# First batch of a gated-attention and MoE kernel: u of all chunks from SyncE's queue, W1's second fourth held back behind chunk 2's attention

## Chip, cores, metric

One core of a Trainium2 chip. The metric is the device time of one execution in microseconds (us); the kernel is tuned, and TensorE is busy 99% of its span.

## The reference

```python
B, S, D, DQK = 8, 3008, 256, 64
scores = (1 / S) * z @ z.T                  # per batch
out = u * (maximum(scores, 0) ** 2 @ v)     # gated attention
x = out.reshape(B * S, D)
h = x @ w_in                                # 256 x 2048
y = (h * sigmoid(1.702 * h)) @ w_out        # 2048 x 256
```

## The kernel before

A batch is worked through in six chunks of 512 rows: scores, ReLU on ACT, square on VectorE, then attention on TensorE. As the scores are symmetric, a square that one chunk has made is transposed by a DMA (into `tt`) for use in another chunk. "The transposes of (m, n)" are squares made for chunk m's rows and chunk n's columns. Chunk 4's attention of the first batch is mixed with the first up-projection (`hg`), which needs W1 in fp16.

```python
pu = tile_pool(name="pu", bufs=2)         # u as loaded, u as turned
pa = tile_pool(name="pa", bufs=1)         # squares "a" (26 buffers), transposed "tt" (14)

def load_u(b, i):
    eng = pool if b or i else sp          # chunk 0 of batch 0 from SyncE, the rest from POOL
    ...
    for k in range(P // QW):              # 4 DMAs of 128 KB
        eng.dma_start(uq[...], src[...])

def turn_u(b, i):                         # VectorE, in order with its squares
    dve.transpose(ut, UQ.pop((b, i)))     # the gate multiplies attention by ut

def turn_unit(b, i, jp, a):               # SyncE, in order
    sp.dma_start_transpose(TT[b, i, cj][...], a)

def load_w(k):
    if k == 0:                            # POOL waits here until chunk 1's gate is made
        hold = const.tile([P, 1], F16, name="hold")
        pool.tensor_copy(hold, XT[0, 1][:, 0, :1])
    if k < 4:                             # 512 KB, a fourth of W1
        WS[k] = pw.tile([P, NCC, DFF // 4], F32, name="wst", tag="y")   # two buffers
        pool.dma_start(WS[k], moe_w_in...)
    ...

# (chunk, step of its attention): what is issued there
LOAD0 = {(1, 14): 2, (2, 12): 3, (2, NJ + 20): 4, (4, 8): 5}           # chunks of u
LOADW = {(2, 16): 0, (2, 30): 1, (3, 9): 2, (3, 41): 3, ...}           # W1, W2
CASTW = {(3, 8): 0, (3, 40): 1, (4, 8): 2, (4, 14): 3}                 # ACT, W1 to fp16
```

POOL and SyncE each issue in order and stop at the first DMA whose buffer or data is not ready: from 14 to 100 us POOL waited 21.5 us for buffers of u, and from 9 to 66 us SyncE waited 23.4 us for squares.

Of the kernel before, what the change touches and what calls it, by code (L numbers as in the profile page):

```python
# [10 lines left out]
F16 = mybir.dt.float16  # L11
P = 128
# [3 lines left out]
def kernel(  # L16
# [39 lines left out]
    dve, act, pe, sp, pool = nc.vector, nc.scalar, nc.tensor, nc.sync, nc.gpsimd  # L56

    const = ctx.enter_context(tc.tile_pool(name="const", bufs=1))
# [20 lines left out]
    ZT, V16, UQ, UT, XT, unit, TT = {}, {}, {}, {}, {}, {}, {}  # L79
# [41 lines left out]
    def first_cast(g, by_act=False):  # L121
        m = g % CB * CB
        for c in range(2):
            dst, src = ZT["st"][g // CB][:, m:m + CB, c, :], ZT["f"][g // CB][:, m:m + CB, :]
            if by_act:
                act.activation(dst, src, AF.Copy, scale=1.0)  # L126
            else:
                dve.tensor_copy(dst, src)

    def first_zt(g):  # L130

        z2 = ZT["st"][g // CB][:, g % CB * CB:(g % CB + 1) * CB]
        zp = ZP[g] if g in ZP else ps1.tile([P, CB, P], F16, name="zp", tag="ps1")
        for k in range(CB):
            pe.transpose(zp[:, k, :], z2[:, k, :, :], ident)  # L135

        def copies():
            zt = ZT[0][:, g * CB:(g + 1) * CB, :].rearrange("d n p -> d (n p)")
            nb = CB if g < NCH - 1 else CB - 1
            dst = zt[:, :nb * P].rearrange("d (p n) -> d p n", n=nb)  # L140
            src = zp[:, :nb, :].rearrange("d n p -> d p n")
            if g in (0, 2, 3):
                act.activation(dst, src, AF.Copy, scale=1.0)  # L143
            else:
                dve.tensor_copy(dst, src)
            if nb < CB:
                dve.tensor_copy(zt[:, nb * P:], zp[:, nb, :])

        return copies


    def load_z(b):
        ZT[b] = pz.tile([P, NJ, P], F16, name="ZT", tag="ZT")
        for n0 in range(0, NJ, NU):
            zst = pw.tile([P, NU, 2, DQK], F16, name="zst", tag="y")
            full = min(NU, NJ - 1 - n0)
            src = z[b, n0 * P:(n0 + full) * P].rearrange("(n p) d -> p n d", p=P)
            pool.dma_start(zst[:, :full, 0, :], src)
            if full < NU:
                for h in range(2):  # L160
                    pool.dma_start(zst[h * SREM:(h + 1) * SREM, full, 0, :], z[b, S0:S])
            pool.tensor_copy(zst[:, :, 1, :], zst[:, :, 0, :])
            sp.dma_start_transpose(ZT[b][:, n0:n0 + NU], zst.rearrange("p n c d -> p (n c d)"))
# [21 lines left out]
    def width(i):  # L185
        return CH if i < NCH - 1 else LAST

    def load_u(b, i):
        eng = pool if b or i else sp
        n = width(i)  # L190
        uq = pu.tile([P, CH // QW, QW, NCC], F32, name="uq", tag="uq")
        src = u[b, i * CH:i * CH + n].rearrange("(q t) c -> t q c", t=QW)
        for k in range(P // QW):
            cs = slice(k * NCC * QW, (k + 1) * NCC * QW)
            eng.dma_start(uq[k * QW:(k + 1) * QW, :n // QW].rearrange("t q c k -> t q (c k)"), src[:, :, cs])  # L195
        UQ[b, i] = uq

    def turn_u(b, i):
        n = width(i)
        ut = pu.tile([P, NCC, CH // QW, QW], F32, name="ut", tag="ut")  # L200
        UT[b, i] = ut
        dve.transpose(
            ut[:, :, :n // QW, :].rearrange("p k q t -> p q k t"),
            UQ.pop((b, i))[:, :n // QW].rearrange("p q c k -> p q k c"),
        )
# [114 lines left out]
    def full(b):  # L320

        return NCH - 2 if b < B - 1 else NCH - 1
# [106 lines left out]

    def load_w(k):  # L430

        if k == 0:
            hold = const.tile([P, 1], F16, name="hold")
            pool.tensor_copy(hold, XT[0, 1][:, 0, :1])
        if k < 4:
            WS[k] = pw.tile([P, NCC, DFF // 4], F32, name="wst", tag="y")
            pool.dma_start(WS[k], moe_w_in.rearrange("(p k) f -> p k f", k=NCC)[:, :, k * DFF // 4:(k + 1) * DFF // 4])
        else:
            fs = slice((k - 4) * CB, (k - 3) * CB)
            pool.dma_start(W2[:, fs], moe_w_out.rearrange("(fo p) c -> p fo c", p=P)[:, fs])  # L440

    def cast_w(k):
        act.activation(W1[:, :, k * DFF // 4:(k + 1) * DFF // 4], WS.pop(k), AF.Copy, scale=1.0)  # L443
# [154 lines left out]
    def pieces(b, i):  # L598
# [22 lines left out]
    LOAD0 = {(1, 14): 2, (2, 12): 3, (2, NJ + 20): 4, (4, 8): 5}  # L621
    TURN = {(1, NJ + 4): 2, (2, NJ + 4): 3, (4, NJ + 4): 4, (5, 8): 5}
    LOADW = {
        (2, 16): 0, (2, 30): 1, (3, 9): 2, (3, 41): 3, (4, 28): 4, (4, 34): 5, (4, 40): 6, (5, 0): 7,
    }
    CASTW = {(3, 8): 0, (3, 40): 1, (4, 8): 2, (4, 14): 3}
    LOAD = {(3, NJ + 20): 4, (4, NJ + 5): 5}
# [13 lines left out]
    def take(b, n):  # L641
        for post_ in scores(b, [queue.pop(0) for _ in range(n)]):
            post_()

    def fill(b):
        assert not queue
        queue.extend(u_ for i in range(NCH) for u_ in pieces(b, i))
# [24 lines left out]
    keep_warm(1)  # L672
    copies()
    ZP[3] = ps1.tile([P, CB, P], F16, name="zp", tag="ps1")
    load_u(0, 1)

    for b in range(B):
        nup = NCH * NFG
        more = b + 1 < B
        sched = SCHED0 if b == 0 else SCHED if more else SCHED_LAST  # L680
        turn, load = (TURN, LOAD) if b else (TURN0, LOAD0)
        head = 0
        for i in range(NCH):
            host = b + 1 if more and i == NCH - 1 else b
            if host > b:
                fill(host)
                LATE.append(host)
            for n, step in enumerate(attend(b, i, b == 0 and i < 2)):
                if b == 0 and i == 0 and n == 5:
                    load_u(0, 0)  # L690
                if b == 0 and i == 0 and n == 2:
                    copies = first_zt(3)
                if b == 0 and i == 0 and n == 3:
                    copies()
                if b == 0 and i == 0 and n in FIRST_CAST:
                    first_cast(FIRST_CAST[n], True)
                if b == 0 and i == 0 and n in FIRST_ZT:
                    first_zt(FIRST_ZT[n])()
                if (i, n) in turn:
                    turn_u(b, turn[i, n])  # L700
                if i == 3 and n in (3, 26) and LAST2:
                    LAST2.pop(0)()
                if (i, n) in load:
                    load_u(b, load[i, n])
                if b == 0 and (i, n) in CASTW:
                    cast_w(CASTW[i, n])
                if b == 0 and (i, n) in LOADW:
                    load_w(LOADW[i, n])
                if more and (i, n) == (NCH - 2, 2 if b else 16):
                    load_z(b + 1)  # L710
                if b == 0 and i == NCH - 1 and n in (8, 30, 42):
                    wsums.pop(0)()
                take(host, sched[i].get(n, 0))
                if i == full(b) and n >= HEAD and (n - HEAD) * LAGY // (2 * NJ - 10) >= head and head < LAGY:
                    up_group(b, head)
                    head += 1
                step()
        late.sort(key=lambda t: t[0])
        if more:
            for i in range(2):  # L720
                load_u(b + 1, i)
            for n0 in range(0, NJ, VB):
                load_v(b + 1, n0)
        prods = products(b)
        for q in range(head, nup):
            if more and q in (head + 14, head + 20):
                k = int(q == head + 20)
                turn_u(b + 1, k)
                load_u(b + 1, k + 2)
            up_group(b, q)  # L730
            if b == 0 and q == head + 3:
                wsums.pop(0)()
            product(b, *prods.pop(0))
            if q >= 30 and q % 2 and late:
                late.pop(0)[1]()
        steps = [lambda kp=kp: product(b, *kp) for kp in prods]
        for step in steps:
            step()
            for sum_ in [SUMS.pop(0) for _ in range(min(len(SUMS), 1 + (len(SUMS) > 4)))]:
                sum_()  # L740
            for _, turn_it in [late.pop(0) for _ in range(min(len(late), 1 + (len(steps) < 10)))]:
                turn_it()
        LATE.clear()
        if more:
            while late:
                late.pop(0)[1]()
            take(b + 1, 2)
# [30 lines left out]
```

## Time and profile before

| | us |
|---|---|
| median of 6 executions (range) | 1180.55 (1180.33 to 1186.32) |
| the profiled execution | 1180.55, span 1178.7 |
| TensorE idle from 14 to 100 us | 0.24 |

Five of the six lie within 0.31 us of each other and one is 5.7 us longer. The lines of the profile that carry the reading stand in the prediction. One more is needed for what comes later. It is the view of the source line that issues the transposes, from 14 to 80 us: the shortest, median and longest time from issue to landing.

```profile
DMA to landing us min/median/max: 3.1/5.2/8.9
```

### The profile page before, as it was taken

How to read it: one execution, taken by the hardware profiler on the slowest of the kernel's cores; microseconds unless marked ns; L12 is line 12 of the kernel's file. 1: busy time of each engine (PE TensorE's matmuls, PEld its weight loads, DVE VectorE, ACT ScalarE, POOL GpSimd, SP SyncE). 2: the span in 40 equal slices, each digit the busy share in tenths (PEclk: the TensorE clock that was granted, in tenths of full speed). 3: DMA queues.
4: the chain of work that ended last, by engine and by line, in shares of the span. 5: the costliest groups of instructions: out<-in, count | busy, mean ns of one | idle time of the engine just before them, and what ended most of it. 6: DMA issues, size and time to landing. Idle time of an engine off the chain costs nothing.

```text
span 1178.7 us, 23495 instructions
## 1 busy us (share of the span) xinstructions
PE 1172.5 (99%) x9238; PEld 667.2 (57%) x9238; DVE 870.7 (74%) x1455; ACT 849.6 (72%) x1033; POOL 222.1 (19%) x313
## 2 busy tenths in 40 slices
PE   9999999999999999999999999999999999999998
PEld 3446664466644675446654467544674446744566
DVE  6779866878758786587875878658786587764776
ACT  7888874688746887478864787647876478772785
POOL 5243101231012310132101431014100241001000
PEclk9999999999999999999999999999999999999999
DMA  9998679877698677976879668896578965796023
GB/s 226 217 120 125 133 116 160 91 112 135 106 156 100 108 135 130 150 91 95 147 128 149 94 93 157 139 137 94 94 135 135 141 106 97 127 158 127 1 37 73
DMA packets 449696, 143.66 MB, mean 122 GB/s; under 512 B 414640, under 2 KB 443056, under 8 KB 449584
## 3 DMA queue, kind: packets, MB, share of 16 engines
q1 hardware_dynamic: 392160, 99.80, 51.2%
q0 software_dynamic: 56064, 41.04, 23.1%
q8 instruction: 72, 1.18, 0.4%
q10 hardware_dynamic: 1360, 1.31, 0.4%
q14 instruction: 40, 0.33, 0.1%
HBM read 60.29 MB, written 24.64 MB: 72 GB/s over the span
## 4 chain that ended last, share of the span: by engine, by line
PE 99%; ACT 1%; issue 0%; DVE 0%
PE o L358 40%; PE hg L399 27%; PE st L523 23%; PE sc L235 6%; PE st L526 1%; PE yp L497 1%; PE w L99 0%; ACT rl L256 0%; ACT W L443 0%; ACT gf L407 0%; PE zp L135 0%; ACT ZT L143 0%; ACT zst L126 0%; DVE y L544 0%; DVE nil L75 0%
## 5 line engine op out<-in xcount | busy, mean ns | idle before, releaser
L407 ACT ACTIVATE gf<-hg 128x1024 f32<-128x1024 f32 (+1 forms) x384 | 385.5, 1004 | 113.6 <-PE hg L399 98.3
L256 ACT ACTIVATE rl<-sc 128x1024 f16<-128x1024 f32 (+1 forms) x301 | 287.5, 993 | 145.4 <-PE sc L235 101.2
L358 PEld LDWEIGHTS <-V 64*128 64x128 f16 (+1 forms) x4052 | 217.7, 94 | 253.9 <-issue 11.8
L399 PE MATMUL hg<-xt,W 128*128 128x512 f16 (+1 forms) x1408 | 354.6, 374 | 0.2
L358 PE MATMUL o<-a,V 64*128 64x512 f16 (+3 forms) x2240 | 296.0, 368 | 0.0
L411 DVE TENSOR_SCALAR gt<-gf 128x1024 f16<-128x1024 f32 (+1 forms) x288 | 203.0, 705 | 114.0 <-ACT gf L407 112.8
L195 POOL DMA_DIRECT2D uq<-in_u_dram x188 | 125.2, 674 | 751.8 <-PE sc L235 527.5
L270 DVE TENSOR_TENSOR a<-rl 128x1024 f16<-128x1024 f16 (+1 forms) x266 | 177.6, 670 | 112.3 <-ACT rl L256 111.0
L358 PE MATMUL o<-tt,V 64*128 64x512 f16 (+1 forms) x1510 | 232.2, 377 | 0.0
L399 PEld LDWEIGHTS <-W 128*128 128x128 f16 x1536 | 149.4, 98 | 125.6 <-issue 2.6
L523 PEld LDWEIGHTS <-WT 128*128 128x128 f16 x1472 | 139.1, 98 | 45.1
L523 PEld LDWEIGHTS <-W 128*128 128x128 f16 x1104 | 104.7, 98 | 32.2
L235 PE MATMUL sc<-ZT 64*128 64x512 f16 (+3 forms) x688 | 115.5, 357 | 0.5 <-ACT ZT L143 0.3
L409 ACT ACTIVATE gt<-gf 128x1024 f16<-128x1024 f32 (+1 forms) x96 | 98.9, 1030 | 3.0
L540 ACT ACTIVATE y<-st 128x256 f32<-128x256 f32 x192 | 70.8, 369 | 35.7 <-PE st L523 29.2
L523 PE MATMUL st<-gt,WT 128*128 128x256 f16 (+1 forms) x736 | 91.9, 268 | 0.0
L523 PE MATMUL st<-s,WT 128*128 128x256 f16 (+1 forms) x736 | 90.8, 268 | 0.0
L523 PE MATMUL st<-gt,W 128*128 128x256 f16 (+1 forms) x736 | 90.8, 268 | 0.0
L544 DVE SCALAR_TENSOR_TENSOR y<-st,y 128x256 f32<-128x256 f32 (+1 forms) x144 | 57.7, 407 | 24.3 <-ACT y L540 11.7
L375 DVE TENSOR_TENSOR xt<-o,ut 128x512 f16<-128x512 f32 x80 | 51.3, 683 | 28.5 <-PE o L358 28.5
L477 DVE TENSOR_TENSOR s<-s,gt 128x1024 f16<-128x1024 f16 (+1 forms) x96 | 63.7, 663 | 1.1
L475 DVE TENSOR_TENSOR s<-gt 128x1024 f16<-128x1024 f16 (+1 forms) x96 | 63.3, 660 | 0.0
(59 smaller groups left out, 668.5 us busy)
## 6 DMA issues: line engine op xcount, KB each, us to landing
uq<-in_u_dram POOLq DMA_DIRECT2D x156, 128.0 KB, 3.6
out_dram<-yo SPq DMA_DIRECT2D x156, 128.0 KB, 2.8
V<-in_v_dram POOLq DMA_DIRECT2D x35, 256.0 KB, 6.4
tt<-a SPq DMA_TRANSPOSE x232, 3.4
uq<-in_u_dram POOLq DMA_DIRECT2D x32, 112.0 KB, 5.4
out_dram<-yo SPq DMA_DIRECT2D x28, 96.0 KB, 6.0
wst<-in_moe_w_in_dram POOLq DMA_DIRECT2D x4, 512.0 KB, 6.2
vst<-in_v_dram SPq DMA_DIRECT2D x3, 512.0 KB, 5.4
```

Of the source, the lines that this page charges most:

```text
L195: eng.dma_start(uq[k * QW:(k + 1) * QW, :n // QW].rearrange("t q c k -> t q (c k)"), src[:, :, cs])
L235: pe.matmul(sc[:, r, :q1 - q0], zt[h, 2 * kp + r, :], zt[h].rearrange("d n p -> d (n p)")[:, q0:q1], start=True, stop=True,)
L256: act.activation(rl[:, :, :n], sc[:, :, :n], AF.Relu, scale=csc)
L270: dve.tensor_tensor(a[:, :, :n], rl[:, :, :n], rl[:, :, :n], ALU.mult)
L358: ins = pe.matmul(acc[c][:, :n], V16[b][h, j].rearrange("p (c k) -> p k c", k=NCC)[:, c], weights(b, i, j)[h], start=(k, m) == first[c], s ...
L399: pe.matmul(hg[:, e, :n], W1[:, c, ff * P:(ff + 1) * P], XT[b, i][:, c, :n], start=(c == 0), stop=(c == NCC - 1),)
L407: act.activation(gf[:, :, :n], hg[:, :, :n], AF.Gelu_apprx_sigmoid, scale=1.0 / FSC)
L409: act.activation(g, gf[:, :, :n], AF.Copy, scale=FSC)
L411: dve.tensor_scalar(g, gf[:, :, :n], FSC, None, ALU.mult)
L477: dve.tensor_tensor(s_, ST[b, k, "S1", h], a11, ALU.subtract)
L523: pe.matmul(bank, right[:, ff], lhs()[:, f], start=first, stop=last, skip_group_check=True)
L540: act.activation(y[:, c, :, o], bank, AF.Copy, scale=1.0 / FSC)
```

## The change

The intent: put u, like the transposes, on SyncE's queue, and keep W1's second fourth off the DMA engines while chunk 2's transposes run, so that these land sooner.

```diff
 def load_u(b, i):
-    eng = pool if b or i else sp
+    eng = pool if b else sp
...
-    if k == 0:
-        hold = const.tile([P, 1], F16, name="hold")
-        pool.tensor_copy(hold, XT[0, 1][:, 0, :1])
+    if k < 2:
+        hold = const.tile([P, 1], F16, name=f"hold{k}")
+        pool.tensor_copy(hold, XT[0, k + 1][:, 0, :1])
...
-    (2, 16): 0, (2, 30): 1, (3, 9): 2, (3, 41): 3, ...
+    (2, 16): 0, (3, 0): 1, (3, 9): 2, (3, 41): 3, ...
...
-load_u(0, 1)                       # ahead of all attention
...
-    if b == 0 and i == 0 and n == 5:
-        load_u(0, 0)
+    if b == 0 and i == 0 and n in (5, 24):
+        load_u(0, n // 24)         # chunk 1 at step 24 of chunk 0
```

More of the change, by code (lines that the diff above doesn't have):

```diff
@@ L623 @@
     LOADW = {
-        (2, 16): 0, (2, 30): 1, (3, 9): 2, (3, 41): 3, (4, 28): 4, (4, 34): 5, (4, 40): 6, (5, 0): 7,
+        (2, 16): 0, (3, 0): 1, (3, 9): 2, (3, 41): 3, (4, 28): 4, (4, 34): 5, (4, 40): 6, (5, 0): 7,
     }
```

## The prediction

> **What bounds the kernel now.** I first read the page's busy times and the chain that ended last. They name one engine.
>
> ```profile
> PE 1172.5 (99%) x9238; PEld 667.2 (57%) x9238; DVE 870.7 (74%) x1455; ACT 849.6 (72%) x1033; POOL 222.1 (19%) x313
> ...
> PE 99%; ACT 1%; issue 0%; DVE 0%
> PE o L358 40%; PE hg L399 27%; PE st L523 23%; PE sc L235 6%; PE st L526 1%; PE yp L497 1%; PE w L99 0%; ACT rl L256 0%; ACT W L443 0%; ACT gf L407 0%; PE zp L135 0%; ACT ZT L143 0%; ACT zst L126 0%; DVE y L544 0%; DVE nil L75 0%
> ```
>
> TensorE is busy for 1172.5 of 1178.7 us and makes up 99% of the chain; no DMA appears in it. So a change of DMA queues can pay only where TensorE waits for a DMA today. The change touches the first batch alone, some 100 us, so I then asked for the busy time by stretch: start-up, the stretch in which the changed loads are issued, the rest.
>
> ```profile
> 0.00:14.00 14.00, 12.30 (x62) 4.53 (x63) 7.58 (x16) 9.68 (x15) 7.65 (x15) 1.00 0.93 289
> 14.00:100.00 86.00, 85.76 (x592) 37.23 (x591) 68.86 (x107) 71.31 (x76) 34.73 (x48) 1.00 1.06 167
> 100.00:1179.00 1079.00, 1074.39 (x8588) 625.48 (x8586) 794.24 (x1334) 768.58 (x944) 179.70 (x252) 1.00 0.73 116
> ```
>
> The columns after the length are PE, PEld, DVE, ACT and POOL busy us, then the granted clock, the DMA share and GB/s. From 14 to 100 us TensorE idles 86.00 - 85.76 = 0.24 us. The DMA engines are full there (share 1.06), yet TensorE doesn't feel it. As busy time could hide stretched matmuls, I also took the distance from each matmul's start to the next in the timeline and compared it with 0.213 us for a full 512-column one (half for one of a pair of 64-row ones). Most of what is over that, about 0.2 us each, is at changes from 64-row to 128-row matmuls, which the change keeps. The waits are five: 0.16 us at 27.9, 0.25 at 54.2, 0.21 at 56.7, and 0.28 each at 68.9 and 72.0 us. They add to 1.2 us, and those that I can name follow an ACT instruction, a cast of W1 or an eviction, not a DMA. No wait of TensorE on a DMA is listed for 14 to 100 us.
>
> Then I read the queues that the change rearranges.
>
> ```profile
> 17.21 2.71 POOL L195 DMA_DIRECT2D uq<-in_u_dram  x4
> 22.72 2.58 POOL L195 DMA_DIRECT2D uq<-in_u_dram  x4 [2.80 <-DVE ut L202]
> 34.63 2.58 POOL L195 DMA_DIRECT2D uq<-in_u_dram  x4 [9.33 <-DVE ut L202]
> ...
> 44.63 0.71 POOL L437 DMA_DIRECT2D wst<-in_moe_w_in_dram  x1 [4.79 <-PE sc L235]
> 48.23 2.61 POOL L195 DMA_DIRECT2D uq<-in_u_dram  x4 [2.88 <-DVE ut L202]
> ...
> 14.19 2.16 SPq L195 DMA_DIRECT2D uq<-in_u_dram  x4
> 16.45 45.97 SPq L298 DMA_TRANSPOSE tt<-a  x20
> ...
> SPq L298 <- DVE a L270: 23.4, 11, 7.2
> ```
>
> On POOL the loads of u stand between W1's; on SyncE 20 transposes fill 16.45 to 62.42 us. Its waits for squares take 23.4 us between 9 and 66 us. Instruction by instruction SyncE is free from 19.15 to 25.56 and from 35.12 to 37.04, then issues without a gap to 62.42, although one transpose costs 1.23 to 1.3 us: some take 2.1 to 4.3. It has fallen some 10 us behind: the square that the transpose at 49.79 reads was made at 39.13.
>
> **What the Trainium skill says.** "DMA: Bandwidth & Descriptors", section "Issuing engines are not separate DMA queues": all issuers end on the same 16 DMA engines, and another issuer only saves sequencer time. The share of 1.06 agrees that there is no spare capacity to find by moving u. The same page's "Rules for kernel authors" says of a transpose next to ordinary DMAs that it "needs nothing". For correctness this kernel agrees; for time the trace shows more. Transposes beside SyncE's own u load (issued at 11.58 and 16.45) landed after 4.7 and 4.1 us; those issued at 17.78 and 38.37, beside POOL's loads, after 8.9 and 8.0. "SBUF — State Buffer", section "SBUF: two separate sides", says that VectorE can lock GpSimd out of writing descriptors for its DMAs, and that a DMA from SyncE escapes this. Here POOL's u DMAs take a steady 0.65 us, so I count nothing for it. "Perfetto Trace Analysis", section "Identifying the Most-Contended Engine", warns that matmul busy time is a poor measure; hence the start-to-start distances above.
>
> **The change part by part.** The order of TensorE, ACT and VectorE is the same in both kernels. Only POOL and SyncE differ: 20 DMAs of u (chunks 1 to 5) leave POOL for SyncE, and a copy of one column holds W1's second fourth.
>
> *POOL* loses 20 DMAs of about 0.65 us = 13 us of issue. POOL is 19% busy and on no path, so this gives 0. The first fourth of W1 was already held until chunk 1's gate, at 39.1 us, and stays there.
>
> *SyncE* gains 20 x 0.54 us (2.16 us for four today) = 10.8 us. It had 23.4 us of waits, but the place counts:
> - chunk 1 goes behind the transpose that ends at 19.15, into the idle stretch to 25.56: 2.2 us, free. It lands before about 25 us (today 27.1); VectorE turns it at 33.1.
> - chunk 2 goes behind the transpose that ends at 35.12: 2.2 us in a gap of 1.9, so 0.3 us of delay. It lands near 40; it is turned at 46.7.
> - chunk 3 goes behind the transposes of chunk pair (2, 4). Those end at 53.86 today; at that pace u would be issued by 56.3 and, with 3.4 us to landing as SyncE's u has today, be there at about 59.8, against a turn at 59.36. This is the tightest. But chunk 3's load no longer sits among the transposes at 34.6 to 40.8, nor W1's second fourth at 44.6 to 50.2. With two of the stretched transposes (2.7 to 4.2 us) back at 1.3, SyncE gains 3 to 4 us, u lands at about 56, and the margin is 3 us.
> - chunks 4 and 5 follow at about 60 and 67, and are turned at 81.3 and 92.6: free.
>
> The transposes have slack in their readers too: those of (1, 2), issued at 25.56 to 29.6, are read near 39.8; those of (2, 3), issued from 37.04 and landed by 46.4, near 54; those of (3, 4), landed by 61.9, near 71. A delay of 2.2 us is hidden 2 to 4 times over. VectorE reuses the squares' buffers, so it waits for landings as well; the nearest that I found is 0.6 us (landed 53.97, used 54.53), and there SyncE should be earlier, not later.
>
> *W1.* The second fourth moves from 44.63 to behind chunk 2's gate, whose first half is made at 51.54 to 52.22: issue near 52.7. Four W1 loads take a median of 6.2 us to landing, so 58.9; its cast runs at 61.56, a margin of 2.7 us. The third fourth waits for the first cast and stays near 53.9, now right behind another 512 KB; with 2 to 3 us on top of today's 60.2 it lands at 63 and is cast at 68.31. The fourth waits for the second cast and keeps 62.91.
>
> Sum on the path: 0 from POOL, 0 from SyncE, 0 from W1, and -0.2 us if one of the small waits goes with the smoother DMA. 1180.64 - 0.2 = 1180.4 us.
>
> **The rivals.** (a) *DMA contention was costing TensorE time, and removing it pays.* For: full DMA engines, transposes stretched to 4.3 us, and a spread of 1180.62 to 1186.32 that a late transpose might explain. Against: 0.24 us idle in 86. All five waits together are 1.2 us, so at most 1179.4.
> (b) *SyncE, in order, falls further behind.* If interference keeps its pace, chunk 3's u is 1 to 2 us late at 59.36; VectorE stands still, the squares behind it are late, and TensorE is about to enter the up-projection, where it follows ACT closely. Against: 23.4 us of waits in the queue. Cost: 1 to 2 us, 1182 us.
> (c) *W1's second fourth is late for its cast.* Two fourths back to back share the engines with transposes; more than 9 us to landing instead of 6.2 would stall ACT at 61.56, and the table load and the first GELU follow with little slack. Cost: what is over 2.7 us, up to 2 us, 1182.5 us.
>
> **Range and chances.** 1180.4, with (a) at the low end (1179) and (b) or (c) at the high end (1182.8). I widen it little, as the two close runs before differ by 0.02 us, and one of three was 5.7 us longer. To be faster by 2% it would have to save 23.6 us, twenty times all waits that I can find; to be slower by 2%, a wait would have to appear in each later batch too, which the change doesn't touch. Faster 0.005, same 0.985, slower 0.01.
>
> **What would show it.** Right: from 14 to 100 us TensorE is busy within 0.5 us of 85.76; POOL issues no u before 93 us; transposes land in 4 to 6 us, with none near 9, and SyncE ends its last tt transpose by about 66 us; the turn of chunk 3 follows the square before it with no wait for a DMA; W1's cast near 61.6 waits for nothing. Wrong: VectorE's turn or ACT's cast waiting for a DMA (b, c), with TensorE idle between 59 and 75 us; or a span shorter by over 1.2 us, which would mean that I misread where TensorE waits.

## The result, and the profile after

Median 1181.36 us of 6 executions (1180.27 to 1182.9), before 1180.55. Ratios here are the mean time of one kernel's runs over that of the other's of the same rounds, so not quite the ratio of the medians. This one is 1.0001, with a 95% interval of 0.9982 to 1.0019: no difference in the mean. Executions over 1.5% slower than the fastest of the same kernel are left out of the means.

The six executions are not one cluster, though: 1180.27, 1180.58 and 1180.58, then 1182.13, 1182.25 and 1182.9. Three are as long as the kernel before at its usual, three are 1.6 to 2.4 us longer. The profile of this first set fell on one of the short ones (1180.58). Its busy time by stretch, with columns as in the prediction:

```profile
14.00:100.00 86.00, 85.76 (x594) 37.28 (x593) 69.19 (x106) 71.28 (x76) 21.96 (x30) 1.00 1.09 167
```

TensorE is busy for the same 85.76 us as before, to the hundredth. POOL has lost 12.8 us of work, and nothing came of it. The queues in order of time, POOL first, then SyncE (start, length, what, how often):

```profile
38.31 0.19 POOL L434 COPY hold<-xt 128x1 f16<-128x1 f16 x1 [21.34 <-DVE xt L375]
38.55 0.85 POOL L437 DMA_DIRECT2D wst<-in_moe_w_in_dram  x1
52.01 0.18 POOL L434 COPY hold<-xt 128x1 f16<-128x1 f16 x1 [12.60 <-DVE xt L375]
52.56 0.73 POOL L437 DMA_DIRECT2D wst<-in_moe_w_in_dram  x1 [0.37 <-ACT rl L256]
53.59 0.72 POOL L437 DMA_DIRECT2D wst<-in_moe_w_in_dram  x1 [0.31 <-ACT W L443]
...
36.76 14.48 SPq L298 DMA_TRANSPOSE tt<-a  x8
51.28 2.19 SPq L195 DMA_DIRECT2D uq<-in_u_dram  x4
53.58 5.00 SPq L298 DMA_TRANSPOSE tt<-a  x2
58.63 5.56 SPq L195 DMA_DIRECT2D uq<-in_u_dram  x4
64.31 4.92 SPq L298 DMA_TRANSPOSE tt<-a  x2
```

W1's second and third fourths, 9.3 us apart before (44.63 and 53.88), are now issued 1 us apart: 1 MB in a row. SyncE is ahead of the kernel before until 51.23 (before, the same eight transposes ended at 53.86). From there on those two loads of W1 are under way: u of chunk 4 takes 5.56 us to issue where u of chunk 3 took 2.19, and the last pair of transposes, (4, 5), is issued at 64.31 and 67.78 where it was 59.81 and 61.15. Landings, from issue:

```profile
DMA to landing us min/median/max: 3.2/3.4/10.2
```

The typical transpose is faster (3.4 us for 5.2), as was meant, and the slowest is slower (10.2 for 8.9). Two margins have shrunk. VectorE's turn of chunk 3 waited 0.31 us for u's last quarter, which landed at 59.44 behind W1's second fourth (58.61). And (4, 5), which TensorE wants near 74.6 us, landed at 71.15; before it was 64.22. The margin went from about 10 us to 3.5. What the longer executions wait for had to be caught in other profiles.

### The profile page after: what moved, and what is told of

The parts are those of the page before. It is cut to its first block, busy times and chain, and to the rows that moved or that the text cites. A ratio compares the mean times of both kernels' runs of the same rounds, so it can differ in the third digit from the quotient of the medians.

```text
span 1178.8 us, 23489 instructions
## 1 busy us (share of the span) xinstructions
PE 1172.3 (99%) x9238; PEld 667.2 (57%) x9238; DVE 870.1 (74%) x1455; ACT 849.3 (72%) x1033; POOL 207.4 (18%) x294
## 4 chain that ended last, share of the span: by engine, by line
PE 98%; ACT 1%; DMA 0%; issue 0%; DVE 0%
PE o L358 40%; PE hg L399 28%; PE st L523 23%; PE sc L235 6%; PE st L526 1%; PE yp L497 1%; ACT rl L256 0%; DMA tt<-a 0%; PE w L99 0%; ACT W L443 0%; ACT gf L407 0%; ACT ZT L143 0%; PE zp L135 0%; ACT zst L126 0%; DVE y L544 0%
## 5 line engine op out<-in xcount | busy, mean ns | idle before, releaser
L411 DVE TENSOR_SCALAR gt<-gf 128x1024 f16<-128x1024 f32 (+1 forms) x288 | 200.2, 695 | 114.9 <-ACT gf L407 114.3
L195 POOL DMA_DIRECT2D uq<-in_u_dram x168 | 111.0, 668 | 737.2 <-PE sc L235 528.1
```

Of the source, the lines that this page charges most:

```text
L195: eng.dma_start(uq[k * QW:(k + 1) * QW, :n // QW].rearrange("t q c k -> t q (c k)"), src[:, :, cs])
L411: dve.tensor_scalar(g, gf[:, :, :n], FSC, None, ALU.mult)
```

## The experiments

Twelve runs were made in three groups, each group on a chip of its own; the kernel before ran 11 times in each group. "Long" below is an execution over 1182.0 us, a line drawn by hand after the runs; some of the expectations were put with 1181.3, and where that changes the answer it is said.

| group | kernel | n | median | mean | range | long | ratio, 95% |
|---|---|---|---|---|---|---|---|
| 1 | before | 11 | 1180.55 | 1181.42 | 1180.00 to 1185.32 | 2 | |
| 1 | after_again | 6 | 1181.59 | 1182.00 | 1180.17 to 1185.37 | 3 | 1.0004, 0.9986 to 1.0022 |
| 1 | u_only | 5 | 1180.39 | 1180.40 | 1179.91 to 1180.91 | 0 | 0.9991, 0.9974 to 1.0007 |
| 1 | w_only | 6 | 1183.57 | 1186.15 | 1180.42 to 1198.73 | 3 | 1.0004, 0.9981 to 1.0028 |
| 1 | u3_early | 6 | 1181.13 | 1181.84 | 1180.11 to 1184.18 | 2 | 1.0003, 0.9985 to 1.0021 |
| 2 | before | 11 | 1181.90 | 1182.46 | 1180.41 to 1184.87 | 5 | |
| 2 | u_only_again | 5 | 1181.06 | 1181.01 | 1180.61 to 1181.49 | 0 | 0.9988, 0.9974 to 1.0002 |
| 2 | u4_late | 6 | 1181.30 | 1181.44 | 1180.23 to 1182.38 | 2 | 0.9992, 0.9978 to 1.0007 |
| 2 | u_only_u4_late | 6 | 1181.49 | 1181.46 | 1180.41 to 1182.70 | 1 | 0.9992, 0.9979 to 1.0005 |
| 2 | u3_late | 6 | 1187.70 | 1187.79 | 1186.65 to 1189.22 | 6 | 1.0045, 1.0032 to 1.0059 |
| 3 | before | 11 | 1181.01 | 1181.23 | 1180.34 to 1183.97 | 1 | |
| 3 | before_again | 6 | 1181.25 | 1182.08 | 1180.42 to 1184.98 | 3 | 1.0007, 0.9993 to 1.0021 |
| 3 | w_only_again | 6 | 1181.78 | 1183.42 | 1180.35 to 1189.09 | 2 | 1.0019, 0.9996 to 1.0041 |
| 3 | w_on_sp | 5 | 1182.19 | 1182.87 | 1182.03 to 1184.12 | 5 | 1.0012, 0.9999 to 1.0025 |
| 3 | u_only_third | 6 | 1180.76 | 1181.31 | 1180.17 to 1184.61 | 1 | 1.0001, 0.9988 to 1.0013 |

One of w_only's three long ones, 1198.73, is slow by the rule of 1.5% and is not in its ratio; it is in the median and mean here. Only u3_late differs from the kernel before with its whole interval; the rest must be read from what the profiles caught.

### after_again: the changed kernel unaltered

> The changed kernel unaltered, to see how often an execution is some 1.9 us longer (3 of 6 so far, at 1182.1 to 1182.9 against 1180.3 to 1180.6). Theory L (chunk 3's u, in SyncE's queue behind the transposes of (2, 4), sometimes lands too late for VectorE's turn at 59.4 us): again 3 to 7 of 10 executions near 1182, and if the profile catches one, VectorE's turn of chunk 3 waits 2 us or more for u. Rival W (W1's second fourth, held back, lands too late for its cast): the same times, but then ACT's cast near 61 us waits. Rival C (chance, nothing to do with the change): 0 or 1 of 10 longer, or the kernel before has as many.

Three of six were long, as in the first set. The profile caught one of them, 1182.61 us. The turn of chunk 3 waited 0.36 us, no more than in the short execution, and no cast of W1 waited. So neither theory L nor W holds as it was put. Rival C, chance, stays open: the kernel before had 2 of 11. The waits of TensorE from 14 to 100 us, in us in total, times, longest:

```profile
PE o L358 <- DMA tt<-a: 1.8, 1, 1.8
```

In order of time, TensorE and then SyncE's queue:

```profile
74.08 0.38 PE L358 MATMUL o<-tt,V 128*128 128x512 f16 x1
76.27 0.38 PE L358 MATMUL o<-tt,V 128*128 128x512 f16 x1 [1.81 <-DMA tt<-a]
...
53.21 5.49 SPq L298 DMA_TRANSPOSE tt<-a  x2
58.74 8.87 SPq L195 DMA_DIRECT2D uq<-in_u_dram  x4
67.72 4.66 SPq L298 DMA_TRANSPOSE tt<-a  x2
```

TensorE stands for 1.81 us, which is most of the added time (1182.61 - 1180.58 = 2.03), and it stands for the transposes of (4, 5). These were issued from 67.72 and landed at 76.23. Ahead of them, u of chunk 4 took 8.87 us to issue. Ahead of that, the transposes of (3, 4), issued at 53.21, landed at 67.42, 0.12 us after W1's third fourth (issued 53.29, landed 67.30). Their 14.2 us are the slowest landing of that stretch:

```profile
DMA to landing us min/median/max: 3.2/3.8/14.2
```

The new theory was then: the hold-back puts two fourths of W1 in a row, and the transposes behind them are late. One reading of the two traces doesn't fit it. From 62 to 66 us, first the short execution, then this one (the last three columns are clock, DMA share and GB/s):

```profile
62.00:66.00 4.00, 4.00 (x25) 1.74 (x22) 2.57 (x7) 3.97 (x6) 0.72 (x1) 1.00 0.90 166
62.00:66.00 4.00, 4.00 (x25) 1.69 (x20) 2.61 (x7) 3.97 (x6) 0.72 (x1) 1.00 1.20 70
```

The two fourths stand in a row in both, yet here the DMA engines, no less busy, moved 70 GB/s instead of 166. So the row of loads alone doesn't decide, and what slowed the engines isn't shown.

### u_only and w_only: each half of the change alone

The edits, with the holds put in words:

```diff
 # u_only: the changed kernel with
+    if k == 0: hold behind chunk 1 alone
-    (2, 16): 0, (3, 0): 1,
+    (2, 16): 0, (2, 30): 1,
 # w_only: the kernel before with
-    if k == 0:
+    if k < 2: hold behind chunk k + 1
-    (2, 16): 0, (2, 30): 1,
+    (2, 16): 0, (3, 0): 1,
```

> u on SyncE's queue, W1's second fourth as in the kernel before. Theory L: the longer executions stay or are more frequent, 1180.3 to 1183, since W1's second fourth is again among the transposes at 44 to 50 us and pushes chunk 3's u back by 2 to 3 us. Rival W: none over 1181. Rival C: no difference from the kernel before.

> W1's second fourth held back, u on POOL's queue as in the kernel before. Theory L: none over 1181, median 1180.5. Rival W: 3 to 7 of 10 near 1182. Rival C: no difference from the kernel before.

u_only was even: 5 of 5 within 1.0 us, none long. This speaks against theory L, which had expected it to be as bad as the changed kernel; rival W had expected none over 1181, as it was. Its turn of chunk 3 waited longer, 0.77 us, and TensorE felt nothing of it. (4, 5) landed at 70.58.

w_only was the worst: three of six at 1186.24, 1190.09 and 1198.73, where theory L had expected none over 1181. The profile caught the one of 1190.09. Waits from 50 to 86 us:

```profile
DVE a L270 <- DMA tt<-a: 5.5, 1, 5.5
ACT W L443 <- DMA wst<-in_moe_w_in_dram: 4.0, 1, 4.0
PE hg L399 <- ACT rl L256: 3.9, 1, 3.9
PE o L358 <- DMA tt<-a: 2.0, 2, 1.7
```

W1's second fourth, issued at 53.19, landed at 65.91, so ACT stood at its cast for 4.0 us: the prediction's rival (c), by name. At the same time VectorE waited 5.5 us for a transpose to free a buffer of squares. TensorE stood for 3.9 us, until the ReLU behind that cast was done (66.90 to 67.80), and for 2.0 us more at transposes, 1.71 of them at (4, 5). That is 5.9 us of the 9.5 that it was longer than 1180.55. The rest stands in the profile's clock, which gives one of the columns here (PEclk, ahead of the DMA share):

```profile
68.00:70.00 2.00, 2.00 (x6) 0.68 (x5) 2.00 (x6) 1.71 (x3) 2.00 (x4) 0.50 1.17 211
70.00:72.00 2.00, 2.00 (x6) 0.69 (x5) 0.88 (x2) 0.77 (x1) 0.54 (x1) 0.50 1.06 265
72.00:74.00 2.00, 2.00 (x7) 0.80 (x6) 0.21 (x1) 1.02 (x1) 0.00 (x0) 0.61 1.37 135
```

TensorE was granted half its clock, by the trace from 66.74 us, still in the stall, to 73.56. It ran again from 67.85, so 5.7 us at half speed cost another 2.9 us: 5.9 + 2.9 = 8.8 of the 9.5.

### u3_early: chunk 3's u earlier

```diff
-LOAD0 = {(1, 14): 2, (2, 12): 3, ...}
+LOAD0 = {(1, 14): 2, (1, 30): 3, ...}
```

> The changed kernel with chunk 3's u ahead of the transposes of (2, 3), right behind chunk 2's u: it should be issued by 38 us and land by 42. Theory L: none over 1181, median 1180.3 to 1180.5, and no wait of the turn of chunk 3. Rival W: still 3 to 7 of 10 near 1182, as W1 isn't touched. Rival C: no difference from the changed kernel.

u of chunk 3 was there by 42.97 us and its turn waited for nothing, and still two of six were at 1184. The profile caught one: TensorE waits 1.95 us for the transposes of (4, 5), which landed at 77.49. So theory L fails: what stretched the executions that the profiles caught is not chunk 3's u. The 1.95 us are not all of it either: this execution is 3.6 us over 1180.55, began some 0.5 us later (the same ReLU starts at 35.77 us here and at 35.27 in the kernel before), and TensorE waited 0.73 us more for a transpose in the last batch, at 1084 us.

### u3_late: what a late u would cost

```diff
-LOAD0 = {(1, 14): 2, (2, 12): 3, (2, NJ + 20): 4, ...}
+LOAD0 = {(1, 14): 2, (2, NJ + 16): 3, (2, NJ + 20): 4, ...}
```

> The changed kernel with chunk 3's u moved behind the transposes of (3, 4), so that it is issued near 54 us, behind two fourths of W1. It measures rival (b) of the prediction: VectorE's turn of chunk 3 (59.4 us) should wait 4 to 8 us for u, and as squares and gates stand behind it in order, every execution should be 2 to 6 us longer, 1182.5 to 1186.5. If a late u costs nothing, as VectorE's lead hides it: within 0.5 us of the changed kernel's executions.

All six were long, from 1186.65 to 1189.22, just above the 1182.5 to 1186.5 that was expected; the median is 5.8 us over that of the kernel before in its group. From 50 to 86 us:

```profile
PE hg L399 <- ACT rl L256: 4.4, 1, 4.4
DVE ut L202 <- DMA uq<-in_u_dram: 5.8, 1, 5.8
```

Of 5.8 us of wait on VectorE, 4.4 reach TensorE: some 1.4 us are hidden. The clock was halved here too, from 65.34 to 72.17 us by the trace; TensorE ran again from 67.77, so this cost another 2.2 us. Rival (b) was real as a mechanism, and a late u has room for about 1.4 us.

### u_only_again and u_only_third

No edit against u_only.

> u on SyncE alone, a second time. The theory is now: the held-back second fourth of W1 is issued right before the third, 1 MB on POOL's queue, and the transposes of (3, 4) and (4, 5) land only behind them, so that TensorE waits near 76 us for (4, 5). Without the hold-back the two loads stand 9 us apart: none of 6 executions over 1181.3, and no wait of TensorE for a DMA near 76 us. Rival: the tight 5 of 5 of the first time were luck, as the kernel before also has some near 1185; then 2 or more of 6 over 1181.3.

> u on SyncE alone, a third time, as it has been the most even (10 of 10 within 1.0 us on each of two chips). Again all within 1.1 us of its shortest, and a mean 0.5 to 1.5 us under that of the kernel before of the same rounds. If that evenness was luck, one or more of 6 is over 2 us above its shortest.

The second time 5 of 5 were within 0.9 us, where the kernel before had 5 of 11 long; one, 1181.49, was over the 1181.3 that none should pass. The third time one of six was at 1184.61, and the mean, 1181.31, was no lower than that of the kernel before (1181.23), so the third expectation fell: 16 executions in all, one long. No profile caught that one. In the third profile (1180.94 us):

```profile
PE hg L399 <- ACT rl L256: 1.0, 1, 1.0
DVE ut L202 <- DMA uq<-in_u_dram: 2.4, 1, 2.4
```

Chunk 3's u had landed at 61.40, 0.2 us behind a fourth of W1, and of 2.4 us of wait 1.0 reached TensorE, in keeping with the 1.4 us of room above. So u_only has a weak spot of its own. (4, 5) landed at 69.39 and 70.58.

### u4_late, and u_only_u4_late as a candidate for the best

```diff
-LOAD0 = {(1, 14): 2, (2, 12): 3, (2, NJ + 20): 4, (4, 8): 5}
+LOAD0 = {(1, 14): 2, (2, 12): 3, (4, 4): 4, (4, 8): 5}       # chunk 4's u behind (4, 5)
```

> The changed kernel with chunk 4's u moved from ahead of the transposes of (4, 5) to behind them on SyncE's queue; W1 is untouched. If what TensorE waits for near 76 us is (4, 5) stuck behind that load, these transposes land by 72 us in the profile, and none of 6 executions is over 1181.3. If W1's two fourths alone make (4, 5) late, whatever stands between, 2 or more of 6 stay near 1182.

> Both mends: u on SyncE, W1's second fourth as in the kernel before, chunk 4's u behind the transposes of (4, 5). The version that should have no long execution at all: all of 6 within 1179.9 to 1181.0, median 1180.3. Under the rival (luck) 1 or 2 of 6 are over 1181.3.

The first half of the expectation held: (4, 5) landed at 66.41 us in u4_late, and at 64.60 in u_only_u4_late, with no wait of TensorE near 76. The second half didn't: two of six and one of six were over 1182, and three and four over 1181.3, on a chip where the kernel before had five of eleven over 1182 and seven over 1181.3. Both profiles are of short executions (1181.15 and 1180.71), so whether the wait near 76 is gone in the long ones too isn't shown; if it is, the spread has other causes as well. The profile of u4_late (span 1179.4) shows one wait that came instead: W2, loaded on POOL behind z, comes late for VectorE's sums. From 86 to 100 us:

```profile
DVE WT L449 <- DMA W<-in_moe_w_out_dram: 2.2, 1, 2.2
ACT rl L256 <- DVE a L270: 1.6, 2, 1.0
PE sc L235 <- ACT rl L256: 0.7, 2, 0.4
```

Of 2.2 us on VectorE, 0.7 reach TensorE. Whether this is what the executions at 1182.3 had, no profile shows. The candidate is not shown to beat the kernel before, nor u_only.

### before_again: the kernel before against itself

> The kernel before against itself, to learn what its own long executions (3 of 11 over 1181.3 on one chip, 7 of 11 on another) wait for. Theory: loads on POOL's queue (there u as well as W1) hold back SyncE's transposes in the first batch, so if the profile catches an execution that is over 1 us long, TensorE, VectorE or ACT waits for a landing (a transpose, u or W1) before 100 us. Rival: its spread has nothing to do with the first batch; then a long profile has the added time after 100 us, or before 14 us. The ratio should be 1 within its interval.

The profile caught a long execution (1184.98). TensorE at that place, and its clock:

```profile
74.61 0.38 PE L358 MATMUL o<-tt,V 128*128 128x512 f16 x1
77.47 0.38 PE L358 MATMUL o<-tt,V 128*128 128x512 f16 x1 [2.48 <-DMA tt<-a]
...
77.00:79.00 2.00, 1.53 (x6) 0.63 (x6) 0.16 (x1) 0.15 (x1) 1.53 (x2) 0.87 0.03 8
79.00:81.00 2.00, 2.00 (x6) 0.76 (x5) 1.09 (x2) 0.88 (x1) 1.71 (x3) 0.50 0.89 69
81.00:83.00 2.00, 2.00 (x8) 0.79 (x7) 0.31 (x2) 1.02 (x1) 0.00 (x0) 0.78 1.55 187
```

It is the same wait at the same place: (4, 5) landed at 77.43, in a kernel without the hold-back, where the first profile of it had 64.22. So the second theory was too narrow. Two fourths of W1 in a row aren't needed for a late (4, 5). That the loads of u on POOL's queue do it here is argued; no run separates them from the rest. The added time again adds up: 2.48 us of wait, and 3.41 us at half clock (78.46 to 81.88 by the trace), which cost 1.7, are 4.2 of the 4.4 us by which it is longer than 1180.55.

### w_only_again

No edit against w_only.

> W1's second fourth held back, u on POOL, a second time. Theory (the hold-back puts two fourths back to back and makes transposes late): 3 or more of 6 executions over 1182, some over 1186, the widest spread of the four kernels of this call. Rival (the first time was chance): the same spread as the kernel before in this call.

Two of six were over 1186 (1186.99 and 1189.09), and the other four from 1180.35 to 1181.82. The widest spread of its group, as the theory had it, but "three or more over 1182" was not reached. The profile fell on the shortest, where (4, 5) landed at 69.01 and nothing waited near 76.

### w_on_sp: u and W1 all on SyncE's queue

```diff
-    if k < 2: hold ...
-        pool.dma_start(WS[k], ...)
+        sp.dma_start(WS[k], ...)
-    (2, 16): 0, (3, 0): 1, (3, 9): 2, (3, 41): 3,
+    (1, 36): 0, (2, 16): 1, (3, 9): 2, (3, 41): 3,
```

> u and W1 all on SyncE's queue, W1's fourths placed by their order among the transposes, no hold. Nothing on POOL's queue moves data from 14 to 68 us. If the long executions come from two queues taking turns around the transposes, each transpose should land 3 to 5 us after its issue with none over 6 where no engine queue is full, no engine waits over 0.5 us for a landing from 14 to 90 us, and all 6 executions lie within 0.8 us of the shortest of the kernel before. If it is the amount of data that is too much, transposes are late here too, TensorE waits near 76 us, and 2 or more of 6 are longer by 1.5 us or more.

Half right. (4, 5) landed at 66.67, the median transpose took 3.8 us, and TensorE waits for no transpose before 100 us; but the slowest took 7.6 us, over the 6 that was put (the other profiles have 7.3 in u3_late to 15.5 in w_only). And all five executions were long, for a reason of the experiment's making: the third fourth stands behind (4, 5) on SyncE, was issued at 64.91 and landed at 70.37. From 50 to 86 us:

```profile
PE hg L399 <- ACT W L440: 2.1, 1, 2.1
ACT W L440 <- DMA wst<-in_moe_w_in_dram: 1.9, 1, 1.9
```

The cast waits 1.9 us, and TensorE 2.1. The shortest of the five is 1.7 us over the shortest of the kernel before in its group. Whether one queue would end the spread is open, and nothing here says that it does: three executions lie at 1182.0 to 1182.2, two at 1183.9 and 1184.1. The profile caught one of the two, and in it TensorE waited another 0.84 us for a transpose in the last batch, at 1084 us.

### What the profiles say together

| profile of | hold-back | (3, 4) landed | (4, 5) landed | TensorE waits for (4, 5) | profiled us |
|---|---|---|---|---|---|
| before | no | 61.9 | 64.2 | 0 | 1180.55 |
| before_again | no | 65.2 | 77.4 | 2.48 | 1184.98 |
| after | yes | 64.8 | 71.2 | 0 | 1180.58 |
| after_again | yes | 68.3 | 76.2 | 1.81 | 1182.61 |
| u3_early | yes | 69.6 | 77.5 | 1.95 | 1184.11 |
| u_only | no | 62.4 | 70.6 | 0 | 1180.91 |
| u_only_again | no | 61.8 | 69.4 | 0 | 1180.61 |
| u_only_third | no | 63.3 | 70.6 | 0 | 1180.94 |

TensorE wants (4, 5) at 74 to 76 us in all of these. The landing moves by up to 13 us between two executions of the same kernel (those of the kernel before, from two sets of runs). Of the profiles left out, (4, 5) landed between 64.6 and 71.1 us in five, with no wait, and in w_only, which was 7 us behind by then, at 84.02 with a wait of 1.71 us.

Two things stand beside this. Three long executions can be compared with a short one of the same kernel, and each has 4 us in which the DMA engines moved under half as much, at a DMA share of 1.15 to 1.26: 70 GB/s for 166 from 62 to 66 us (after_again, after), 123 for 280 (before_again, before) and 111 for 304 (w_only, w_only_again) from 54 to 58 us. Over 53 to 68 us it is 139 for 204, 191 for 203 and 159 for 236, so in before_again it was short. And (4, 5) is not the only wait that comes and goes: in the last batch, from 1080 to 1085 us, TensorE waited 0.46 to 0.84 us for a transpose in u_only_again, after_again, u3_early and w_on_sp, 0.17 in after; the other profiles list none.

## Why the prediction was right, and where it wasn't

The time was right: 1181.36 lies in the range of 1179.0 to 1182.8, and "within 2%" was certain by its own argument. The point, 1180.4, is what the shorter half of the executions takes; the other half is longer by about 1.9 us, so that the median is a time between the two, and that it is in the range says little. The prediction's account of where such a loss would come from was partly wrong.

- *TensorE waits for no DMA, so nothing is to be won*: right. 85.76 us of 86 both before and after, in the short execution; the median landing of a transpose fell from 5.2 to 3.4 us, below the 4 to 6 that was put, and the time didn't follow.
- *POOL loses 20 DMAs, worth 0*: right.
- *W1's second fourth is issued near 52.7 and lands at 58.9; the third lands at 63*: 52.56, 58.61 and 63.36 in the short execution. In the long one the third took until 67.30. Its cast, at 68.02 in the short execution, still didn't wait.
- *SyncE gains 3 to 4 us by the time it reaches chunk 3's u*: 2.6 us (51.28 against 53.86). *u lands at about 56, with a margin of 3*: wrong. Three of its four parts landed by 55.8, the last at 59.44 behind W1's second fourth. The margin was -0.3, and it was free because, as u3_late shows, about 1.4 us of lateness are hidden.
- *A delay of 2.2 us is hidden 2 to 4 times over*: the step that failed. Its list of readers stopped at (3, 4) and left out (4, 5), the last in the queue, where all delays of SyncE add up. They were issued 6.6 us later (67.78 for 61.15), not 2.2, and landed 6.9 us later. I had counted u's issue at 0.54 us a DMA; chunk 4's four took 5.56 us in the short and 8.87 us in the long execution, for 2.16, while W1's third fourth was still landing (63.36 and 67.30). That W1 is what stopped the queue is argued from these times.
- *SyncE's last tt transpose ends by about 66, none lands after near 9 us*: wrong, 69.2 and 10.2 us, and that in the short execution already.
- *Rival (b)*, SyncE in order falling behind: its mechanism is the one that showed, with 1182 as its time. Its consumer was another: TensorE at (4, 5), not VectorE at chunk 3's u. *Rival (c)*: seen in w_only alone. *Rival (a)*, that the spread before comes from a late transpose: right for the one long execution of the kernel before that a profile caught, though the change didn't cure it.

What stays open: whether the changed kernel has long executions more often than the kernel before. It had 6 of 12, the kernel before 12 of 45 over all groups, u_only 1 of 16 and w_only 5 of 12 (one of them slow), and the chips differ (1 to 5 of 11 for the kernel before). With the line at 1181.3 these are 6 of 12, 17 of 45, 3 of 16 and 7 of 12. The numbers point against the hold-back and for moving u, and the intervals of the means don't settle it. What decides, in one execution, whether a transpose beside POOL's loads lands after 9 or 14 us, and why the DMA engines then move half as much, no run shows either.

## What to carry to other kernels

When an engine with 99% of the chain waits for nothing, a change of the queues around it can win nothing, but it can spend margins: list every reader of every in-order queue that you lengthen, and look at the last one first. Holding a load back doesn't only move it, it also puts it next to the one that follows. And time a kernel often enough to see two clusters; a median of six between them is no time that any execution takes.

## What the Trainium skill lacked or had wrong

- "TensorE: Matmul & The Clock Gate", "Part 1: The HAM clock gate", has the clock halve after one idle window or more, about 3.4 us. Here TensorE had been idle for only 2.48 us (before_again), and it ran at 0.50 for 3.41 us; with 3.9 and 4.4 us (w_only, u3_late) it was halved for 6.83 us, in u3_late from 2.0 us into the stall on (63.37 to 65.34). Waits of 1.81, 1.95 and 2.08 us (after_again, u3_early, w_on_sp) left it at 1.00. So these three stalls cost 1.5 to 1.7 times their length.
- "DMA: Bandwidth & Descriptors", "Rules for kernel authors", says that a transpose next to ordinary DMAs needs nothing. True of the results, which were right in every run; not of the time. A transpose took 3.1 us at best (before), and 14.2 us in after_again beside two 512 KB loads from POOL.
- The same page, "Queues, rings and completion order", has each DMA engine take turns between its queues packet by packet. It doesn't say what that does to a transpose beside a load. From 36 to 70 us of after_again SyncE's queue moved 3.55 MB in 14293 packets and POOL's 2.10 MB in 576, so a packet of POOL's is some 15 times as large; by an estimate from the page's turns, which takes the trace's packets for the page's, so is what POOL's load gets in a turn. A transpose issued 0.08 us before W1's third fourth landed 0.12 us after all its 512 KB, 14 us later, which fits; no run changed the packets.
- No page says how much landings vary from one execution to the next: the same transposes of the same kernel landed at 64.2 and at 77.4 us.
